# One slot body instead of three, and the remainder moved into short conditional blocks at the slot's end

## The chip, the cores and the metric

One core of one Trainium2 chip runs the kernel. The metric is the device time of one execution in microseconds. TensorE does the matmuls and transposes, VectorE, ScalarE and GpSimd the work between them, SyncE issues most of the weight loads. In the profile their names are PE (PEld for its weight loads), DVE, ACT, POOL and SP; a trailing q means the engine's sequencer, which waits, branches, loads registers and issues DMAs.

## The reference, cut to what matters

Causal attention (2 batches, 12 heads, 448 tokens, head size 64), then a mixture of eight experts in which each token goes to one expert, then a second stage that all 896 tokens go through.

```python
attn = softmax(mask(q @ k.T / 8)) @ v            # -> x: 896 tokens x 768
expert_idx = argmax(cos(x, expert_emb) / tau)    # one expert of 8 for each token
gate_w = probability of that expert
for e in range(8):
    mask = expert_idx == e
    if not mask.any(): continue
    h = maximum(x[mask] @ w1[e], 0)              # w1[e]: 768 x 1024
    out[mask] = gate_w[mask] * (h @ w2[e])       # w2[e]: 1024 x 768
x = out
h = maximum(maximum(x @ m1, x @ m2), x @ m3)     # 768 x 768 each
return h @ m_out
```

## The kernel before

The attention is written out by hand in an order of its own (the strings of `SCHEDULE`) and ends with the routing: a few dozen small VectorE operations on counts, ranks and tables, from which the indices for the gathers and the register values of all later branches come.

The expert stage works in slots of 128 tokens of one expert. Slots 0 and 1 are part of the last `SCHEDULE` string, slot 2 always follows, and slots 3 to 11 stand in nested conditions on the number of slots (`rest3` to `rest11`, line 1230). With these inputs there are seven slots, 0 to 6. A slot multiplies fp32 data as pairs of a high and a low fp32r part: `L1` (x by w1, two halves of 512 columns), a ReLU on ScalarE, transposes of the hidden units (`htr`), `L2` (by w2, two halves of 384), and in the next slot the gate (`yev`, ScalarE, into the tile `y`) and the transposes of the result (`ytr`). While a slot runs, `ws` loads the weights of the next slot's expert and splits them into high and low parts (ScalarE and VectorE), each piece in a condition on the register `need`: the split is left out when the next slot has the same expert.

What remains of an expert's tokens after its full slots, if it is 64 or fewer, becomes a light row of 32 or 64 tokens, computed in plain fp32 from the raw weights. A light row rides in a slot of number 3 or more whose successor needs no new weights, since the buffers for raw weights (six of 768 KB) are free there; rows that find no slot go to up to eight tail blocks (`tail0` to `tail7`, line 1224) between slot 2 and slot 3. Here there are three light rows: 32 tokens in slot 3, 64 in slot 4, 32 in slot 6. Slot 5 is plain and loads weights for slot 6. No tail block runs.

Every slot of number 3 or more is written three times (lines 464 to 470): plain, with a light row of 32, with one of 64. `kind`, two bits of a register that `kinds_load` (line 1194) fills from the table `tabi`, chooses. In the two bodies with a light row its steps stand between the slot's own: `begin` issues six of eight weight loads and gathers the tokens; `x` (token transposes) and `L1` stand ahead of the slot's second `L2` group, `hT` and `L2` after later groups, `out` at the end; the last two weight loads are issued inside `Light.L1` and reuse buffers of the first ones. VectorE computes the tables in `lights` (slot 1) and `lights2` (late in slot 2, hook `(2, 0)`, behind all of the splits of w1 and ahead of those of w2).

Branch hints for `rest4` and on are set in the slot before (`rest_hint`). The program on each engine runs in order; conditions and their register arithmetic are instructions of the engine's queue.

Of the kernel before, what the change touches and what calls it, by code (L numbers as in the profile page):

```python
# [37 lines left out]
def kernel(  # L38
# [15 lines left out]
    nc = tc.nc  # L54
# [60 lines left out]
    k64 = const.tile([P, 14], F32, name="k64")  # L115
# [5 lines left out]
    def consts(tp):  # L121
# [10 lines left out]
        nc.gpsimd.iota(k64, pattern=[[64, 14]], base=0, channel_multiplier=0, allow_small_or_imprecise_dtypes=True)  # L132
# [166 lines left out]
    class Slot:  # L299
# [15 lines left out]
        def regs(self):  # L315
            i = self.i
            if self.prep:
                if i:
                    xg(i + 1)
                if i < 3:  # L320
                    self.needs()
# [62 lines left out]
    class Light:  # L384
        def __init__(self, row, nt):
            self.row, self.nt, self.T = row, nt, P // nt
            self.w = {}

        def begin(self):
            r, nt = self.row, self.nt  # L390
            self.e = nc.values_load(tabi[0:1, T_LE + r:T_LE + r + 1], engines=(ET.SP, ET.Pool), min_val=0, max_val=E - 1)
            self.off = nc.values_load(tabi[0:1, T_LO + r:T_LO + r + 1], engines=(ET.Activation,), min_val=0, max_val=896)
            self.load([(0, p) for p in (0, 2, 1, 3)])
            nc.gpsimd.tensor_copy(out=lix, in_=idx[:, bass.ds(self.e + NH, 1)])
            nc.gpsimd.indirect_dma_start(out=lxr[:nt], out_offset=None, in_=xd, in_offset=bass.IndirectOffsetOnAxis(ap=lix[:nt], axis=0))
            nc.gpsimd.tensor_copy(out=lgt, in_=grep[:, self.T // 4, bass.ds(self.e, 1)])
            self.load([(1, p) for p in (0, 2)])

        def load(self, places):
            for kind, p in places:  # L400
# [72 lines left out]
    def slot_body(S, prev, R):  # L473
        if R:
            R.begin()
        elif S.prep and S.i > 2:
            S.needs()
# [901 lines left out]
```

## Time and profile before

| | us |
|---|---|
| median of 3 runs | 505.13 |
| lowest, highest | 504.69, 509.04 |
| the profiled execution | 505.45 |
| its span, first to last instruction | 503.7 |
| mean granted TensorE clock | 0.959 |
| TensorE busy | 460.2 (91%) |
| VectorE, ScalarE busy | 304.6 (60%), 235.9 (47%) |

The profiled execution takes 505.45 us, of which 503.7 us are the span and 1.75 us lie around it. The granted clock is a share of full speed: 1.00 is 2.4 GHz, 0.50 is 1.2 GHz. Busy time doesn't count branches, register loads, semaphore and DMA-issuing instructions; these are in the views by source line, under a q name (TensorE's under PEldq).

### The profile page before, as it was taken

The page shows a single profiled execution, that of the slowest core. Times are in us where ns is not written, and L with a number is a line of the kernel's source. Part 1 is how long each engine was busy: PE and PEld are TensorE (multiplying, and loading weights), DVE is VectorE, ACT ScalarE, POOL GpSimd, SP SyncE. Part 2 cuts the span into 40 slices and gives each one's busy share as a digit, 9 for nine tenths or more (in the row PEclk, how much of TensorE's full clock was granted, in tenths as well). Part 3 has the DMA queues.
Part 4 walks back from the last instruction along what each step waited for, and adds up shares of the span by engine and source line. Part 5 has one row for each costly group of instructions (what it writes and reads, how often), then busy time and mean ns, then how long its engine had stood idle before and what let it go on. Part 6 is the DMA issues. An engine that isn't in the chain of part 4 may idle for free. (4 is left out here: it accounts for less than half of the span.)

```text
span 503.7 us, 8299 instructions
## 1 busy us (share of the span) xinstructions
PE 460.2 (91%) x2801; PEld 384.7 (76%) x2801; DVE 304.6 (60%) x697; ACT 235.9 (47%) x521; POOL 54.9 (11%) x98
## 2 busy tenths in 40 slices
PE   8899999999899949919999597899999999999994
PEld 6666666776789938718679476699999999999994
DVE  5899868985769891100107420689899898844000
ACT  6768779797359943112128331644344443411000
POOL 5330221111101020100001300000000000000111
PEclk9999999999899979958999799799999999999998
DMA  8754427711159949680549642753355430000111
GB/s 211 202 170 108 120 78 289 299 61 39 31 209 391 391 139 350 223 334 8 188 118 375 234 188 112 308 196 135 116 187 173 141 127 0 1 0 33 62 64 62
DMA packets 28618, 81.52 MB, mean 162 GB/s; under 512 B 13432, under 2 KB 14968, under 8 KB 28544
## 3 DMA queue, kind: packets, MB, share of 16 engines
q1 hardware_dynamic: 25648, 71.46, 40.5%
q0 software_dynamic: 2272, 9.05, 5.3%
q8 instruction: 33, 0.54, 0.5%
q14 instruction: 41, 0.34, 0.2%
q10 hardware_dynamic: 624, 0.14, 0.1%
HBM read 75.13 MB, written 5.51 MB: 160 GB/s over the span
## 5 line engine op out<-in xcount | busy, mean ns | idle before, releaser
L1181 PE MATMUL pm<-x2h,dwh 128*128 128x448 f32 x204 | 74.8, 367 | 0.0
L1182 PE MATMUL pm<-x2l,dwh 128*128 128x448 f32 x204 | 74.8, 367 | 0.0
L1183 PE MATMUL pm<-x2h,dwl 128*128 128x448 f32 x204 | 74.7, 366 | 0.0
L1187 PE MATMUL l<-w1h,xhp 128*128 128x512 f32 x73 | 33.7, 462 | 23.1 <-issue 12.1
L629 PE MATMUL pss<-kt,qbd 128*128 128x320 f32 (+6 forms) x168 | 45.8, 395 | 0.9 <-ACT prb L643 0.8
L643 ACT ACTIVATE prb<-pss,sm 128x64 f32<-128x64 f32 (+6 forms) x84 | 39.5, 484 | 9.5 <-DVE sm L636 9.4
L215 DVE TENSOR_TENSOR hl<-htp,hh 128x512 fp32r<-128x512 f32 x11 | 7.6, 689 | 57.0 <-ACT hh L214 48.1
L1183 PEld LDWEIGHTS pm<-x2h,dwl 128*128 128x128 f32 x204 | 38.3, 188 | 3.4
L1181 PEld LDWEIGHTS pm<-x2h,dwh 128*128 128x128 f32 x204 | 38.3, 188 | 3.4
L1182 PEld LDWEIGHTS pm<-x2l,dwh 128*128 128x128 f32 x204 | 38.3, 188 | 3.3
L1187 PE MATMUL l<-w2h,hh 128*128 128x384 f32 x112 | 40.1, 358 | 0.7 <-ACT hh L218 0.7
L1187 PE MATMUL l<-w2l,hh 128*128 128x384 f32 x112 | 38.3, 342 | 0.0
L182 ACT CAST dwh<-dt_t 128x768 fp32r<-128x768 f32 (+1 forms) x20 | 15.5, 773 | 48.1 <-DVE dt_t L181 48.1
L1187 PEld LDWEIGHTS l<-w1h,xhp 128*128 128x128 f32 x73 | 16.1, 220 | 26.3 <-issue 18.6
L629 PEld LDWEIGHTS pss<-kt,qbd 128*128 128x128 f32 x168 | 28.1, 190 | 9.3 <-ACT prb L643 1.8
L253 DVE TENSOR_TENSOR w1l<-raw,w1h 128x768 fp32r<-128x768 f32 x24 | 21.5, 951 | 20.6 <-PE l L1187 17.5
L636 DVE TENSOR_REDUCE sm<-pss 128x1 f32<-128x448 f32 (+6 forms) x84 | 31.3, 412 | 4.1 <-PE pss L632 3.9
L1187 PE MATMUL l<-w1l,xhp 128*128 128x512 f32 x73 | 32.4, 444 | 0.0
L663 PE MATMUL pst<-ident,prb 128*128 128x128 f32 x192 | 30.0, 281 | 2.1 <-DVE prb L653 1.7
L1333 POOL DMA_INDIRECT out_dram<-ob,sidx x7 | 6.8, 977 | 209.3 <-DVE sidx L1178 177.6
L1187 PE MATMUL l<-w2h,hl 128*128 128x384 f32 x112 | 26.9, 344 | 2.0 <-DVE hl L221 2.0
L1181 PE MATMUL po<-woh,h2h 128*128 128x384 f32 (+2 forms) x84 | 28.2, 335 | 0.0
(330 smaller groups left out, 984.8 us busy)
## 6 DMA issues: line engine op xcount, KB each, us to landing
raw<-in_moe_w_dram SPq DMA_DIRECT2D x56, 768.0 KB, 7.0
rawd<-in_moe_w_dram SPq DMA_DIRECT2D x18, 768.0 KB, 4.7
rawd<-in_moe_w_out_dram SPq DMA_DIRECT2D x6, 768.0 KB, 5.0
vr<-in_v_dram SPq DMA_DIRECT2D x12, 256.0 KB, 2.8
kt<-in_k_dram SPq DMA_DIRECT2D x12, 224.0 KB, 4.6
xd<-xall POOLq DMA_DIRECT2D x12, 224.0 KB, 3.2
qbd<-in_q_dram SPq DMA_DIRECT2D x23, 112.0 KB, 4.5
xrp<-xd,idx POOLq DMA_INDIRECT x8, 6.5
```

Of the source, the lines that this page charges most:

```text
L182: nc.scalar.copy(out=hi[:, c0:c1], in_=f)
L215: nc.vector.tensor_tensor(out=lo, in0=ps_ap, in1=hi, op=ALU.subtract)
L253: nc.vector.tensor_tensor(out=lo[:, sl], in0=r[:, sl], in1=hi[:, sl], op=ALU.subtract)
L629: nc.tensor.matmul(ps[:, o:o + n], lhsT=qbd[p % 4][:, i], rhs=ktt[p][:, :n], start=i == SG[g][0], stop=False, skip_group_check=True)
L636: nc.vector.tensor_reduce(out=sms[p][:, 0, SC[i]:SC[i] + 1], in_=held["s", p, g][:, SO[i]:SO[i] + 64 * (i + 1)], axis=AX.X, op=ALU.max, ne ...
L643: nc.scalar.activation(out=prb[p % 2][:, poff[i]:poff[i] + n], in_=ps[:, SO[i]:SO[i] + n], func=AF.Exp, bias=sm[:, 0, SC[i]:SC[i] + 1], sc ...
L663: nc.tensor.transpose(ps[:, n * P:(n + 1) * P], prb[p % 2][:, poff[i] + kt * P:poff[i] + (kt + 1) * P], ident)
L1181: nc.tensor.matmul(o, lhsT=lh, rhs=rh, start=first, stop=False)
L1182: nc.tensor.matmul(o, lhsT=lh, rhs=rl, start=False, stop=False)
L1183: nc.tensor.matmul(o, lhsT=ll, rhs=rh, start=False, stop=last)
L1187: nc.tensor.matmul(o, lhsT=a, rhs=b, start=first and n == 0, stop=last and n == len(ops) - 1)
L1333: nc.gpsimd.indirect_dma_start(out=out, out_offset=bass.IndirectOffsetOnAxis(ap=sidx[:, t:t + 1], axis=0), in_=ob, in_offset=None)
```

## The change

Each slot now has one body. A slot of number 3 or more gets a `Light` object that shares the slot's eight raw buffers. `begin` stands at the slot's start in a condition of its own on SyncE and GpSimd alone (six loads, the gather of always 64 tokens, two copies of gates); the transposes of the tokens (`x`) are done in every such slot, of rows that a memset on GpSimd filled with zeros once; the copy of their result is in a condition on VectorE. The rest moves to the slot's end, behind the last `L2` group: `sizes(L1)`, then `rest` (the last two loads, a condition on SyncE), then `sizes(tail)` (`hT`, `L2`, `out` in a row). `sizes` is a condition on TensorE, ScalarE and VectorE, and in it a choice between 32 and 64 tokens. The slot's own conditional weight splits stay in every body. `kinds_load` loads the register four times, for four groups of engines, and `needs` is loaded in each slot. `lights2` moves from hook `(2, 0)` to `(2, 3)`, ahead of the last four splits of w1. Of the routing's small operations two leave the first chain for `lights`, `g64` halves, and `selL` is new.

```diff
-    k64 = const.tile([P, 14], F32, name="k64")
+    k64 = const.tile([P, 7], F32, name="k64")
...
     class Light:
-        def begin(self):
-            r, nt = self.row, self.nt
-            self.e = nc.values_load(tabi[...T_LE + r...], engines=(ET.SP, ET.Pool), ...)
-            self.off = nc.values_load(tabi[...T_LO + r...], engines=(ET.Activation,), ...)
-            self.load([(0, p) for p in (0, 2, 1, 3)])
-            nc.gpsimd.tensor_copy(out=lix, in_=idx[:, bass.ds(self.e + NH, 1)])
-            nc.gpsimd.indirect_dma_start(out=lxr[:nt], ..., in_=xd, in_offset=...lix[:nt]...)
-            nc.gpsimd.tensor_copy(out=lgt, in_=grep[:, self.T // 4, bass.ds(self.e, 1)])
-            self.load([(1, p) for p in (0, 2)])
+        def begin(self, nt=64):
+            r = self.row
+            for place in self.first:
+                self.w[place] = self.raw_of(*place)
+            with self.ride("s", nt):
+                self.e = nc.values_load(tabi[...T_LE + r...], engines=(ET.SP, ET.Pool), ...)
+                for place in self.first:
+                    wdma(self.e, *place, self.w[place])
+                nc.gpsimd.tensor_copy(out=lix, in_=idx[:, bass.ds(self.e + NH, 1)])
+                nc.gpsimd.indirect_dma_start(out=lxr, ..., in_=xd, in_offset=...lix[:64]...)
+                for t in range(2):
+                    nc.gpsimd.tensor_copy(out=lgt[:, t:t + 1], in_=grep[:, t, bass.ds(self.e, 1)])
+
+        first = [(0, 0), (0, 1), (0, 2), (0, 3), (1, 0), (1, 2)]
+        last = [(1, 1), (1, 3)]
+
+        def rest(self):
+            for place in self.last:
+                self.w[place] = self.raw_of(*place)
+            with self.ride("s"):
+                e = nc.values_load(tabi[...T_LE + self.row...], engines=(ET.SP,), ...)
+                for place in self.last:
+                    wdma(e, *place, self.w[place])
+
+        def ride(self, engines, nt=0):
+            if self.row >= NL:
+                return ExitStack()
+            return tc.If(self.kind(engines) > 0)
+
+        def kind(self, engines):
+            return (rest["k" + engines] // 4 ** self.row) % 4
+
+        def sizes(self, part):
+            ...
+            with tc.If(self.kind("c") > 0):
+                with tc.If(self.kind("c") == 1) as small:
+                    self.nt, self.T = 32, 4
+                    part()
+                with small.Else():
+                    self.nt, self.T = 64, 2
+                    part()

         def x(self):
             pb = bank("t", "lxt", 3)
             for k in range(KD):
-                nc.tensor.transpose(pb[:, k * nt:(k + 1) * nt], lxr[:nt, ...], ident[:nt, :nt])
-            nc.vector.tensor_copy(out=sp["y"][:, :KD * nt], in_=pb[:, :KD * nt])
+                nc.tensor.transpose(pb[:, k * 64:(k + 1) * 64], lxr[:, ...], ident[:64, :64])
+            with self.ride("v"):
+                nc.vector.tensor_copy(out=sp["y"][:, :KD * 64], in_=pb[:, :KD * 64])
...
             nc.scalar.activation(out=hp0[:, :f], in_=pb[:, :f], func=AF.Relu)
-            self.load([(1, p) for p in (1, 3)])
...
+        def tail(self):
+            self.hT()
+            self.L2()
+            self.out()
...
     def slot(i, prep, prev):
-        kind = (rest["k"] // 4 ** (i - 2)) % 4
-        with tc.If(kind == 0, preferred_fallthrough_block=True) as plain:
-            slot_body(S, prev, None)
-        with plain.Else():
-            with tc.If(kind == 1, preferred_fallthrough_block=True) as small:
-                slot_body(S, prev, Light(i - 2, 32))
-            with small.Else():
-                slot_body(S, prev, Light(i - 2, 64))
+        slot_body(S, prev, Light(i - 2, S.raw_of) if i > 2 else None)
...
     def slot_mid(S, R=None):
...
-        if R:
-            R.x()
         S.L2(0, range(4))
         S.htr(1)
         hook(i, -1)
...
-        if R:
-            R.L1()
-        ws(0, (2, 0), (2, 1))
+        hook(i, 3)
+        S.ws(0, (2, 0), (2, 1))
         S.L2(1, range(4))
-        if R:
-            R.hT()
-        ws(0, (3, 0))
+        S.ws(0, (3, 0))
         S.L2(0, range(4, 8))
-        if R:
-            R.L2()
-            hook(i, 2)
-        ws(0, (3, 1))
+        S.ws(0, (3, 1))
         hook(i, 0)
...
-        ws(1, (0, 0), (0, 1))
+        if R:
+            R.x()
+        S.ws(1, (0, 0), (0, 1))
         S.L2(1, range(4, 8))
-        ws(1, (2, 0), (2, 1), (1, 0), (1, 1), (3, 0), (3, 1))
+        S.ws(1, (2, 0), (2, 1))
+        if R:
+            hook(i, 2)
+            R.sizes(R.L1)
+            R.rest()
+            R.sizes(R.tail)
+        S.ws(1, (1, 0), (1, 1), (3, 0), (3, 1))
         if i == 2:
             hook(i, 2)
-        if R:
-            R.out()
         hook(i, 1)
...
     lxr = lxw[:64]
+    nc.gpsimd.memset(lxr, 0.0)
...
     def kinds_load():
-        rest["k"] = nc.values_load(tabi[...T_KIND...], min_val=0, ...)
+        for g, engines in (("", None), ("c", (ET.PE, ET.Activation, ET.DVE)), ("s", (ET.SP, ET.Pool)), ("v", (ET.DVE,))):
+            kw = {"engines": engines} if engines else {}
+            rest["k" + g] = nc.values_load(tabi[...T_KIND...], min_val=0, ..., **kw)
...
-    hooks[2, 0] = lambda: lights2()
+    hooks[2, 3] = lambda: lights2()
```

## Rows read from the trace of the kernel before

**Rows 1.** Stretches: us, busy us (instructions) of each engine, granted clock, DMA share, GB/s

```profile
178.00:185.10 7.10, 0.11 (x2) 0.02 (x1) 7.00 (x25) 3.81 (x5) 2.10 (x2) 0.81 0.09 35
185.10:213.70 28.60, 28.12 (x227) 22.85 (x227) 6.31 (x12) 5.78 (x13) 4.29 (x8) 0.93 0.78 273
213.70:224.70 11.00, 0.00 (x0) 0.00 (x1) 0.00 (x0) 1.96 (x6) 0.37 (x2) 0.63 0.93 349
224.70:258.50 33.80, 33.77 (x172) 23.94 (x173) 3.56 (x6) 5.08 (x10) 1.17 (x2) 0.92 0.28 101
258.50:277.60 19.10, 19.06 (x107) 17.21 (x105) 10.47 (x14) 13.89 (x24) 2.35 (x3) 1.00 0.86 310
277.60:281.60 4.00, 0.00 (x0) 0.00 (x0) 4.00 (x6) 4.00 (x7) 2.19 (x1) 0.97 0.61 198
281.60:311.50 29.90, 28.88 (x227) 23.34 (x227) 4.82 (x8) 4.87 (x11) 1.77 (x1) 0.89 0.50 193
311.50:317.30 5.80, 0.03 (x2) 0.03 (x1) 0.56 (x2) 1.57 (x6) 0.00 (x0) 0.85 0.02 6
```

**Rows 2.** Branches on TensorE's queue, by source line and window: ns shortest/median/longest, starts

```profile
L464 PEldq COMPARE_BRANCH  x1: 2505/2505/2505, 182.2 to 182.2; - x1
...
L464 PEldq COMPARE_BRANCH  x1: 4432/4432/4432, 212.5 to 212.5; - x1
...
L467 PEldq COMPARE_BRANCH  x2: 386/3861/7336, 211.7 to 217.2; - x2
...
L372 PEldq COMPARE_BRANCH  x1: 6217/6217/6217, 274.3 to 274.3; - x1
...
L1228 PEldq COMPARE_BRANCH  x2: 203/1798/3392, 313.0 to 316.6; - x2
```

**Rows 3.** Stretches in slot 0, columns as in Rows 1

```profile
124.00:127.70 3.70, 1.01 (x6) 0.45 (x4) 3.41 (x18) 1.06 (x2) 0.34 (x11) 1.00 0.00 0
127.70:131.50 3.80, 3.80 (x26) 3.49 (x27) 1.95 (x6) 1.15 (x2) 0.00 (x0) 0.55 0.00 0
```

**Rows 4.** GpSimd's groups by line and form: busy us, mean ns of one

```profile
L570 POOL MEMSET qbd<- 64x448 f32 x6 | 3.0, 493 | 0.2
```

**Rows 5.** VectorE's timeline: start, us, line, operation

```profile
124.15 0.27 DVE L97 TENSOR_TENSOR lxw<-n8p,k 128x112 f32<-128x112 f32 x1
...
176.84 0.45 DVE L97 TENSOR_TENSOR lxw<-enT,v 128x288 f32<-128x288 f32 x1
...
180.51 0.18 DVE L1146 CAST tabi<-tabf 1x56 int32<-1x56 f32 x1
...
206.21 0.42 DVE L432 COPY lhT<-lht 128x256 f32<-128x256 f32 x1 [3.64 <-PE lht L431]
```

**Rows 6.** ScalarE's timeline: start, us, line, operation, [idle before <- what ended it]

```profile
189.34 1.05 ACT L291 ACTIVATE y<-l,gs 128x384 f32<-128x384 f32 x2 [6.93 <-DVEq L1222]
...
203.82 0.38 ACT L424 ACTIVATE hp<-ll 128x256 f32<-128x256 f32 x1 [2.15 <-PE ll L414]
...
211.19 0.42 ACT L443 ACTIVATE hp<-ll,lgt 128x192 f32<-128x192 f32 x1 [6.99 <-PE ll L414]
```

**Rows 7.** Register loads of line 1195 on VectorE's queue: ns, start

```profile
L1195 DVEq TENSOR_LOAD <-tabi x1: 320/320/320, 188.2 to 188.2; - x1
```

**Rows 8.** TensorE's timeline: start, us, line, operation

```profile
193.28 0.82 PE L296 MATMUL ytp<-ident,y 128*128 128x128 f32 x6
...
200.88 2.80 PE L414 MATMUL ll<-raw,y 128*32 128x256 f32 x48
...
208.21 2.81 PE L414 MATMUL ll<-raw,lhT 128*32 128x192 f32 x64
...
240.68 5.37 PE L414 MATMUL ll<-raw,y 128*64 128x512 f32 x24
```

**Rows 9.** SyncE's timeline, the late two loads of slot 3's light row

```profile
202.40 0.91 SPq L247 DMA_DIRECT2D raw<-in_moe_w_dram  x2
```

**Rows 10.** The microsecond in which they finish, columns as in Rows 1

```profile
207.00:208.00 1.00, 1.00 (x8) 0.96 (x6) 0.00 (x0) 0.00 (x0) 0.00 (x0) 1.00 0.72 283
```

More of the change, by code (lines that the diff above doesn't have):

```diff
@@ L319, in regs @@
                     xg(i + 1)
-                if i < 3:
-                    self.needs()
+                self.needs()
         def needs(self):
@@ L399, in load, with __init__ @@
-        def load(self, places):
-            for kind, p in places:
-                self.w[kind, p] = wraw()
-                wdma(self.e, kind, p, self.w[kind, p])
+        def __init__(self, row, raw_of=None):
+            self.row, self.w = row, {}
+            self.raw_of = raw_of or (lambda kind, u: wraw())
+        def begin(self, nt=64):
[3 more added lines that the diff above has]
+            with self.ride("s", nt):
+                self.e = nc.values_load(tabi[0:1, T_LE + r:T_LE + r + 1], engines=(ET.SP, ET.Pool), min_val=0, max_val=E - 1)
+                for place in self.first:
+                    wdma(self.e, *place, self.w[place])
+                nc.gpsimd.tensor_copy(out=lix, in_=idx[:, bass.ds(self.e + NH, 1)])
+                nc.gpsimd.indirect_dma_start(out=lxr, out_offset=None, in_=xd, in_offset=bass.IndirectOffsetOnAxis(ap=lix[:64], axis=0))
+                for t in range(2):
+                    nc.gpsimd.tensor_copy(out=lgt[:, t:t + 1], in_=grep[:, t, bass.ds(self.e, 1)])
@@ new lines @@
+        first = [(0, 0), (0, 1), (0, 2), (0, 3), (1, 0), (1, 2)]
[4 more added lines that the diff above has]
+            with self.ride("s"):
+                e = nc.values_load(tabi[0:1, T_LE + self.row:T_LE + self.row + 1], engines=(ET.SP,), min_val=0, max_val=E - 1)
+                for place in self.last:
[4 more added lines that the diff above has]
+            return tc.If(self.kind(engines) > 0)
@@ new lines, in kind @@
+        def kind(self, engines):
+            return (rest["k" + engines] // 4 ** self.row) % 4
+        def sizes(self, part):
+            if self.row >= NL:
+                self.nt, self.T = 64, 2
+                part()
+                return
+            with tc.If(self.kind("c") > 0):
[3 more added lines that the diff above has]
+                with small.Else():
+                    self.nt, self.T = 64, 2
+                    part()
@@ L475, in slot_body @@
             R.begin()
-        elif S.prep and S.i > 2:
-            S.needs()
         S.L1(0, range(6))
@@ L486, in slot_body @@
         prev.ytr(1)
-        if not R:
-            S.ws(0, (0, 0))
+        S.ws(0, (0, 0))
         S.htr(0)
@@ L493, in slot_mid @@
         i = S.i
-        def ws(*a):
-            if not R:
-                S.ws(*a)
         if i == 1:
-            ws(0, (0, 0))
-        ws(0, (0, 1))
+            S.ws(0, (0, 0))
+        S.ws(0, (0, 1))
         if i > 1:
             S.L1(1, range(3, 6))
-        ws(0, (1, 0))
+        S.ws(0, (1, 0))
         if i > 1:
             S.relu(1)
-        ws(0, (1, 1))
-        if R:
-            R.x()
+        S.ws(0, (1, 1))
         S.L2(0, range(4))
@@ L917 @@
     lix = rtile([P, 1], "lix", I32)
-    lgt = rtile([P, 1], "lgt")
+    lgt = rtile([P, 2], "lgt")
     grep = rtile([P, 2, E], "grep")
@@ L921 @@
     n8 = rtile([P, E], "n8")
-    g64 = lview(160, 112).rearrange("p (e k) -> p e k", e=E)
-    nbs = rtile([P, 2, E], "nbs")
-    nb8, nh8 = nbs[:, 0], nbs[:, 1]
+    g64 = lview(160, 56).rearrange("p (e k) -> p e k", e=E)
+    nh8 = rtile([P, E], "nh8")
     pre8 = rtile([P, E, E], "pre8")
@@ L1224 @@
             es.enter_context(tc.If(rest["k"] >= 4 ** NL * (t + 1), preferred_fallthrough_block=True, label=f"tail{t}"))
-            L = Light(NL + t, 64)
-            for part in (L.begin, L.x, L.L1, L.hT, L.L2, L.out):
-                part()
+            L = Light(NL + t)
+            L.begin()
+            L.x()
+            L.sizes(L.L1)
+            L.rest()
+            L.sizes(L.tail)
     with ExitStack() as es:
```

43 lines of the change are left out of this document (18 added, 25 removed), and 2 rows, old and new, of the table SCHEDULE.

## The prediction

> **What bounds the kernel now.** I read the windows by stage first, for the stretch that the change touches, 178 to 317 us: it begins where TensorE has finished slot 2 and ends where the second stage begins. Look at TensorE's column and at the clock [rows 1]. TensorE is the bound in slot 5 (19.06 of 19.1 us busy) and within the other slots, but four stretches hold almost none of it: 7.1 us ahead of slot 3, 11.0 ahead of slot 4, 4.0 ahead of slot 6, 5.8 ahead of the second stage, 27.9 us in all. Slots 3, 4 and 6 also run at mean clocks of 0.93, 0.92 and 0.89. If the lower level is half speed, the time lost is (1 - clock) x length: 2.0, 2.7 and 3.3 us.
>
> Then the branches by source line say what fills the gaps [rows 2]. The choice of body (L464, L467) held TensorE's queue for 2.5 us ahead of slot 3 and for 4.4 and 7.3 us ahead of slot 4. The jump from the end of the plain body of slot 5 over two unused bodies (under L372) took 6.2 us, of which some 3 lay under matmuls already queued. The exit (L1228) took 3.4 us. A plain body is some 210 TensorE instructions long (107 matmuls and 105 weight loads in slot 5 [rows 1]), one with a light row longer, and these branches jump over one or two of them. A branch of the same kind at 211.7 took 0.39 us and one at the exit 0.2, so the length of a jump is not all: a long branch is taken here as one whose target was not there yet.
>
> The gap ahead of slot 3 has two other late comers. VectorE writes the integer table at 180.5 to 180.7, 3.9 us after it began the tables at 176.84 [rows 5], and TensorE can't know its branches before. And ScalarE's `y` of slot 2, whose transposes TensorE does 8.2 us into slot 3 (193.28 [rows 8]), waits until 189.34 for VectorE to pass the tail blocks [rows 6].
>
> **The change, part by part.** The sum is made against the profiled execution, 505.45 us (span 503.7 and 1.75 around it); the median of the runs, 505.13, is 0.3 lower. Plus is slower.
>
> *Routing.* The memset of 64x768 scales from 64x448 in 0.49 us [rows 4] to 0.85 us, an estimate. GpSimd does it ahead of its other small work there, and the first VectorE write to that tile (`g64`, 124.15 [rows 5]) has to wait for it. Two small operations leave this chain; the smallest row of VectorE here lasts 0.18 us [rows 5], so they give some 0.3 back. The memset ends half a microsecond or so after `g64` could begin: I take +0.3, bounds 0 and +0.9. The three operations added in `lights` lie under TensorE's slot 1 and cost nothing; without that cover they would cost 3 x 0.18.
>
> *Entry of slot 3.* Tables 3.9 us earlier and no choice of body: TensorE's first matmul can come just after 178, say at 179.1 with the added register load. Its work up to the transposes of `y` took 8.2 us, 6.2 without the slow clock, so it stands at them at 185.3. VectorE has the same operations in another order and is busy without a break (7.00 of 7.1 us [rows 1]), so it comes to the tail blocks no earlier, and it has two more register loads of 0.32 us each, 0.4 with what surrounds them [rows 7]. `y` is then begun at 190.1 and transposed from 190.8 instead of 193.28: -2.5. TensorE has waited 5.5 us for it and starts at the low clock again. Even short waits do that: after two gaps that left 1.0 us of work in 3.7, the clock was 0.55 for 3.8 us [rows 3]. So the 2.0 us that slot 3 loses now are lost again, behind the transposes: -0.5 in all, bounds -2.5 and +1. What is late next is VectorE's splitting, and the tables' earlier place buys next to nothing.
>
> *The light rows of 32 (slots 3 and 6).* Today each step stands between groups of the slot's own matmuls. At the end of the slot nothing is left to cover them, and TensorE waits for each hand-over. Behind `L1`: ReLU 0.22 us after the last matmul, 0.38 long, 0.2 back to TensorE, 0.8 [rows 6, 8]. Behind the transposes of `hT`: a copy of 0.42 us, 0.66 with the hand-over [rows 5]. Behind `L2`: the gate, 0.42 us, 0.8 [rows 6]. The last two weight loads: issued at 202.40, half-way through `L1` [rows 8, 9], they moved their last bytes 0.72 into the microsecond from 207 [rows 10], 5.35 us after the issue. In the new body they stand behind a condition, so I let them start when `L1` ends; `L2`, with 0.8 + 0.4 + 0.66 us and its first half of 1.4 ahead of it, needs them after 3.2 us: 2.1 us of waiting. Branch and register instructions not hidden, 0.4. That is +4.8 for each row, bounds +2.7 (loads half-way through `L1`, as now) and +7 (the low clock after it). SyncE's next loads, those of the following slot, queue behind the two late ones, and nobody needs them for 19 us.
>
> *The light row of 64 (slot 4).* `L1` takes 5.37 us [rows 8] and `L2` as long, so the loads come in time (0.15 us of waiting); the three hand-overs are wider, 1.0, 0.9 and 1.0; 0.5 for branches: +3.6, bounds +3 and +5.6.
>
> *Entry of slot 4.* Of 11.0 us 0.5 stays: -10.5. Of 2.7 us of low clock I keep 1.0 for what the chain of slot 3 may leave: -1.7.
>
> *Slot 5 and entry of slot 6.* Token transposes without use, 0.55 us, and branches, 0.4: +1.0. The jump of 6.2 us goes: the gap of 4.0, 1 us of idle time and 2.3 of low clock inside slot 6 go with it, less 0.3 for branches: -7.0. `y` is no limit there: ScalarE, busy to the end of the gap, is through with it 23 us after slot 5 began [rows 1], and TensorE asks for it after 19.1 + 1.0 + 6.2 = 26.3.
>
> *Exit.* The jump from the 32-row body over the 64-row one, ahead of the exit's own jump, goes; the 3.4 us of the exit stay: -1.2, bounds -4.5 (its hint works with fewer jumps between) and 0.
>
> *Joins.* A consumer behind a conditional block waits for the end of the producer's block, not for its instruction. No row shows what that adds; I take a second hand-over of 0.2 us, as above, for three in each of three chains: +1.8, bounds 0 and +3. The unused conditions of `ws` in light slots are on ScalarE, VectorE and SyncE, which idle for most of such a slot (5.78 and 6.31 us busy of 28.6 [rows 1]); in an engine without that slack each would cost its branch.
>
> Sum: 0.3 - 0.5 + 2 x 4.8 + 3.6 - 10.5 - 1.7 + 1.0 - 7.0 - 1.2 + 1.8 = -4.6. That gives 500.9 for a profiled execution, 500.5 against the median.
>
> **The rivals.**
>
> *The skips in slot 5 miss (504.5).* A slot with no light row jumps over the code of `L1` (48 matmuls of the one size and 24 of the other, each with a weight load, 144 instructions) and at once over the tail (about 216 more). Rows show jumps of this length both ways: 0.39 us, and 2.5 to 6.2 [rows 2], the longest while weight loads filled the DMA queues, as they do in slot 5 (share 0.86 [rows 1]). Half of a 6 us hold is hidden by queued matmuls; the rest, and some 2 us of low clock behind it, cost 4 to 5. The Trainium skill ("Runtime: NRT & Kernel Launch", section "Instruction fetch mechanics") says that a taken branch to a target outside the current two pages of 256 instructions stalls for a fetch; by that rule this pair of skips, 360 instructions, leaves the window from a little under half of all positions. The same section gives TensorE room for 2048 instructions, by which none of the long branches should have been; the trace speaks against that figure.
>
> *The chains are short (494).* The two late loads start half-way through `L1` (2 x -2.1), the clock holds, the exit's hint works (-3.4 at most). For it: full clock inside the light rows today. Against it: a condition on SyncE stands between.
>
> *Slower: the chains are bound by the late loads (511).* If the following slot's loads, whose buffers come free at the same moment, share the queues with the two late ones, four loads of 2 us each and the start of 1.3 make them land 9.4 us behind `L1` instead of 5.4: +4 in each of three chains, with 2 us of low clock each, less what the sum holds already: about +10 over the forecast. It decides from the point where `L2`'s second half waits for more than some 3 us. Against it: SyncE issues the late ones first.
>
> *The jumps stay (505).* The conditions at the end of a slot could miss as often as the bodies did. Against it: most of the jumps that are left are a quarter as long.
>
> **How the numbers follow.** Forecast 0.42, with 497 to 503.5 as its own range; skips miss 0.25; short chains 0.18; late loads 0.09; jumps stay 0.06. One per cent is 5 us, about what a measurement of this kernel can tell from no change. Faster by more than that (under 500.1): not quite half of the forecast (0.19), nearly all of the short chains (0.17), a fifth of the missed skips, with cheaper chains (0.05): 0.41. Slower: the late loads and a little of the two cases that end near 505: 0.11. The range takes in most of the short chains and the missed skips: 492 to 508.
>
> **What would show it.** In the profile after: no TensorE branch of over 1 us ahead of slots 3 and 4; slot 3's `y` transposes near 191 with `y` still released by VectorE at the tail blocks; in each light row three idle times of 0.7 to 1.0 us on TensorE, and one of about 2 us in the second half of `L2` of the 32-row ones; slot 4 beginning near 218. I am wrong if the gaps stay, if TensorE runs on through the light rows, or if a skip in slot 5 holds its queue.

## The result and the profile after

The changed kernel takes 502.49 us (median of 20 runs, 498.29 to 507.75) against 506.54 for the kernel before beside it (20 runs, 504.53 to 510.62): ratio 0.990, 95% interval 0.987 to 0.993, 3.7 to 6.4 us less. That ratio leaves out the three slowest runs of the changed kernel (506.35 to 507.75), which are more than 1.5% above its fastest; the two medians alone give 0.992, or 4.1 us less. The prediction said 500.5 against 505.13, or 4.6 less. Timed once more with other kernels the ratio was 0.9925 (0.9895 to 0.9955). The total came out near the forecast. In the profiles the stretch that the prediction is about gave only two thirds of it, though, and a place that it did not look at gave much of the rest; both are shown below.

The changed kernel's profiled execution took 499.93 us (span 498.2), 5.5 less than that of before; it is one of the shorter of its 20 runs. Its stretches, cut where its slots begin and end, in the columns of [rows 1]: us, busy us of each engine, granted clock, DMA share, GB/s.

```profile
178.60:191.60 13.00, 6.72 (x28) 5.02 (x28) 10.28 (x14) 3.89 (x7) 3.79 (x7) 0.98 0.54 187
191.60:203.70 12.10, 12.10 (x65) 11.34 (x65) 2.31 (x4) 4.38 (x9) 1.19 (x2) 0.88 0.79 277
203.70:219.00 15.30, 11.35 (x137) 6.87 (x136) 0.98 (x2) 0.81 (x2) 0.93 (x1) 0.89 0.61 215
219.00:253.00 34.00, 31.59 (x175) 22.14 (x174) 3.56 (x6) 7.16 (x16) 1.66 (x5) 1.00 0.49 180
253.00:274.20 21.20, 19.93 (x112) 17.58 (x110) 12.17 (x16) 14.18 (x24) 3.57 (x5) 1.00 0.57 208
274.20:283.10 8.90, 6.57 (x28) 5.02 (x28) 3.73 (x5) 3.69 (x6) 0.69 (x1) 1.00 0.87 312
283.10:311.30 28.20, 23.60 (x200) 18.09 (x200) 3.86 (x7) 5.10 (x11) 0.00 (x0) 0.88 0.48 188
311.30:314.50 3.20, 0.03 (x1) 0.00 (x0) 0.62 (x2) 1.53 (x6) 0.00 (x0) 0.93 0.19 40
```

The empty stretches of [rows 1] are gone. In their place each slot with a light row has TensorE busy for less than its length, and 283.10 to 311.30 has a clock of 0.88. Cut finer, the low clock of slots 3 and 6 lies in four short stretches: behind the two waits at 191.58 and 283.07 (the first is in the second row above), and at the end of the two light rows of 32.

```profile
215.10:219.00 3.90, 3.27 (x32) 1.62 (x32) 0.00 (x0) 0.42 (x1) 0.00 (x0) 0.57 0.95 364
...
283.10:287.00 3.90, 3.90 (x15) 3.37 (x16) 1.26 (x2) 2.35 (x5) 0.00 (x0) 0.56 1.01 411
287.00:307.30 20.30, 16.43 (x155) 13.11 (x153) 2.60 (x5) 2.33 (x5) 0.00 (x0) 1.00 0.47 182
307.30:311.30 4.00, 3.26 (x31) 1.61 (x31) 0.00 (x0) 0.42 (x1) 0.00 (x0) 0.59 0.03 6
```

TensorE's branches show why the empty stretches went; the groups answer to [rows 2] (ns shortest/median/longest, starts).

```profile
L425 PEldq COMPARE_BRANCH  x4: 68/72/83, 203.9 to 240.0; - x4
...
L426 PEldq COMPARE_BRANCH  x8: 66/187/337, 204.3 to 252.6; - x8
...
L425 PEldq COMPARE_BRANCH  x2: 334/554/773, 270.3 to 273.1; - x2
...
L1249 PEldq COMPARE_BRANCH  x2: 186/322/459, 311.1 to 311.7; - x2
```

No branch lasts 0.8 us where those of [rows 2] lasted 2.5 to 7.3. TensorE's timeline shows what it waits for now, and answers to [rows 8] (start, us, line, operation, [idle before <- what ended it]).

```profile
179.64 0.49 PE L1203 MATMUL l<-w1h,xhp 128*128 128x512 f32 x1 [1.08 <-ACT w2h L252]
191.58 1.54 PE L296 MATMUL ytp<-ident,y 128*128 128x128 f32 x6 [4.80 <-ACT y L291]
...
209.89 0.44 PE L459 MATMUL lht<-ident,hp 128*128 128x128 f32 x2 [0.60 <-ACT hp L453]
210.84 1.51 PE L443 MATMUL ll<-raw,lhT 128*32 128x192 f32 x32 [0.52 <-DVEq L371]
213.17 0.52 PE L443 MATMUL ll<-raw,lhT 128*32 128x192 f32 x4 [0.82 <-DMA raw<-in_moe_w_dram]
215.07 2.78 PE L443 MATMUL ll<-raw,lhT 128*32 128x192 f32 x28 [1.38 <-DMA raw<-in_moe_w_dram]
218.49 0.52 PE L484 MATMUL lyt<-ident,hp 128*64 128x128 f32 x3 [0.63 <-ACT hp L471]
218.97 0.49 PE L1203 MATMUL l<-w1h,xhp 128*128 128x512 f32 x1
...
245.03 0.63 PE L459 MATMUL lht<-ident,hp 128*128 128x128 f32 x4 [0.83 <-issue]
246.45 5.38 PE L443 MATMUL ll<-raw,lhT 128*64 128x384 f32 x32 [0.78 <-DVEq L371]
252.62 0.55 PE L484 MATMUL lyt<-ident,hp 128*128 128x128 f32 x3 [0.79 <-ACT hp L471]
...
274.23 0.49 PE L1203 MATMUL l<-w1h,xhp 128*128 128x512 f32 x1 [1.30 <-PEq L425]
283.07 1.38 PE L296 MATMUL ytp<-ident,y 128*128 128x128 f32 x6 [2.29 <-ACT y L291]
302.52 1.51 PE L443 MATMUL ll<-raw,lhT 128*32 128x192 f32 x32 [0.52 <-DVE lhT L460]
304.99 0.52 PE L443 MATMUL ll<-raw,lhT 128*32 128x192 f32 x4 [0.96 <-SPq L1249]
307.40 2.77 PE L443 MATMUL ll<-raw,lhT 128*32 128x192 f32 x28 [1.90 <-SPq L1249]
314.51 0.74 PE L1203 MATMUL pm<-x2h,dwh 128*128 128x448 f32 x1 [3.19 <-ACT x2h L214]
```

Slot 3 begins at 179.64, stands at `y` until 191.58, and slot 4 begins at 218.97. The hand-overs of the light rows take 0.5 to 0.8 us each; `L2` of 32 rows waits twice in its course for the late loads. The row at 283.07 is a wait that was not forecast: slot 6 stands 2.29 us at the transposes of `y`. SyncE's longest wait for TensorE's queue leads to its cause (us in total, times, longest):

```profile
SPq L247 <- PEq L425: 10.0, 1, 10.0
```

SyncE, in slot 5, wants to issue the last two weight loads for slot 6 (places 1 and 3 of w2) and waits 10.0 us, until 274.05. That is 0.09 us after TensorE's semaphore instruction behind the last jump, the one over the unused tail (273.96). The loads land behind the start of slot 6, and ScalarE splits them before it comes to `y`:

```profile
279.14 1.57 ACT L252 CAST w2h<-raw 128x768 fp32r<-128x768 f32 x2 [6.65 <-DMA raw<-in_moe_w_dram]
280.98 1.56 ACT L252 CAST w2h<-raw 128x768 fp32r<-128x768 f32 x2 [0.26 <-DMA raw<-in_moe_w_dram]
282.45 1.05 ACT L291 ACTIVATE y<-l,gs 128x384 f32<-128x384 f32 x2
```

A ledger by stretch, from the start of the first matmul of each slot in the two traces (the first stretch begins where slot 2's last matmul ends: 178.10 before, 178.56 after). The column "predicted" holds the prediction's terms of that stretch, its joins at 0.6 for each chain. The last is a second profiled execution of the changed kernel, e10 below.

| stretch | before | after | difference | predicted | e10 |
|---|---|---|---|---|---|
| end of slot 2 to slot 4 | 46.63 | 40.41 | -6.2 | -5.6 | 40.44 |
| slot 4 | 33.81 | 34.00 | +0.2 | +2.5 | 34.26 |
| slot 5, to slot 6 | 23.09 | 21.26 | -1.8 | -2.7 | 21.18 |
| slot 6, to the second stage | 35.65 | 40.28 | +4.6 | +0.9 | 40.25 |
| sum | 139.18 | 135.95 | -3.2 | -4.9 | 136.13 |

The remaining -2.7 of the profiled difference lie behind 314.5, in the second stage, whose program the change does not touch; ahead of the end of slot 2 there is +0.5.

### The profile page after: what moved, and what is told of

Read it like the earlier page. It is cut to its first block, busy times and chain, and to the rows that moved or that the text cites. A ratio compares the mean times of both kernels' runs of the same rounds, so it can differ in the third digit from the quotient of the medians.

```text
span 498.2 us, 8666 instructions
## 1 busy us (share of the span) xinstructions
PE 458.9 (92%) x2807; PEld 381.6 (77%) x2807; DVE 305.7 (61%) x699; ACT 236.3 (47%) x521; POOL 53.0 (11%) x102
## 5 line engine op out<-in xcount | busy, mean ns | idle before, releaser
L1203 PE MATMUL l<-w2h,hh 128*128 128x384 f32 x112 | 39.1, 349 | 0.7 <-ACT hh L218 0.7
L1203 PE MATMUL l<-w1h,xhp 128*128 128x512 f32 x73 | 30.6, 420 | 2.8 <-PEq L425 1.3
L1203 PE MATMUL l<-w1l,xhp 128*128 128x512 f32 x73 | 29.4, 403 | 0.0
L1197 PE MATMUL po<-woh,h2h 128*128 128x384 f32 (+2 forms) x84 | 28.2, 335 | 0.0
L1199 PE MATMUL po<-woh,h2l 128*128 128x384 f32 (+2 forms) x84 | 28.1, 335 | 0.0
L1198 PE MATMUL po<-wol,h2h 128*128 128x384 f32 (+2 forms) x84 | 28.1, 335 | 0.0
```

The lines of the kernel that those rows point to most:

```text
L1197: nc.tensor.matmul(o, lhsT=lh, rhs=rh, start=first, stop=False)
L1198: nc.tensor.matmul(o, lhsT=lh, rhs=rl, start=False, stop=False)
L1199: nc.tensor.matmul(o, lhsT=ll, rhs=rh, start=False, stop=last)
L1203: nc.tensor.matmul(o, lhsT=a, rhs=b, start=first and n == 0, stop=last and n == len(ops) - 1)
```

## The experiments

**Tables where they were, in the changed kernel** (e1).

```diff
-    hooks[2, 3] = lambda: lights2()
+    hooks[2, 0] = lambda: lights2()
```

> The changed kernel with the tables computed behind the last four splits of w1 again, as before. My theory (TensorE in slot 3 waits for y, which waits for VectorE at the tail blocks, whatever the order of VectorE's work): TensorE's first matmul of slot 3 comes some 3 us later (about 183), its wait ahead of the y transposes shrinks from 4.8 to about 2 us, the transposes stay within 0.7 us of where they are, and the time is that of the changed kernel within 1 us (ratio to before 0.99). Rival (the earlier tables are a main part of the gain): 3 us more than the changed kernel, ratio 0.996.

Ratio to the kernel before 0.9956 (0.9928 to 0.9984). By the total the tables seem to be worth 0.3 to 0.6%, against the changed kernel's second and first timing, and the ratio is the one that the rival named; the trace puts the difference elsewhere.

```profile
182.74 0.79 PE L1203 MATMUL l<-w1h,xhp 128*128 128x512 f32 x1 [4.49 <-ACTq L1240]
191.18 1.01 PE L296 MATMUL ytp<-ident,y 128*128 128x128 f32 x6
```

Slot 3 starts 3.1 us later than in the changed kernel, at low clock, and its transposes of `y` come at 191.18 without a wait, against 191.58. What the early tables win is lost in waiting for `y`, as the prediction said. The stretch from slot 2 to the second stage takes 137.00 us against 135.95, and 0.9 of the 1.05 us lie at the exit, where TensorE stands still for 4.10 us instead of 3.19; its branch took 3.34 us here and 0.46 in the changed kernel's first profile. The interval overlaps with that of the changed kernel's second timing, so the totals do not decide; the trace speaks for the theory.

**Tables alone, in the kernel before** (e2).

```diff
+        hook(i, 3)
         ws(0, (2, 0), (2, 1))
...
-    hooks[2, 0] = lambda: lights2()
+    hooks[2, 3] = lambda: lights2()
```

> The kernel before with nothing but the tables moved ahead of the last four splits of w1. TensorE still takes the jump to the light body (2.5 us), so slot 3 starts near 181.5 instead of 185.1; y is begun at 189.3 as before, so its transposes come at 190.0 to 190.5 instead of 193.3. My theory: 2 to 3 us less than before there, ratio 0.994 to 0.996; the gaps ahead of slots 4 and 6 as before. Rival (the low clock or VectorE takes all of it back): ratio 1.0.

Ratio 1.002 (0.9992 to 1.0049), the rival's. The transposes of `y` in slot 3 come at 191.45, 1.8 us earlier than [rows 8]; ahead of slot 4 all of it is lost, since the branches there take as long as before or longer:

```profile
L464 PEldq COMPARE_BRANCH  x2: 2565/3853/5141, 179.3 to 211.9; - x2
...
L467 PEldq COMPARE_BRANCH  x3: 78/300/7713, 182.2 to 217.3; - x3
```

So the tables alone gain nothing, and the long branches go only where the bodies go.

**Hints for the choice of body, in the kernel before** (e6): could the long branches have been mended without the change?

```diff
-        with tc.If(kind == 0, preferred_fallthrough_block=True) as plain:
+        with tc.If(kind == 0, preferred_fallthrough_block=True, label=f"plain{i}") as plain:
...
+    def kind_hint(i):
+        k = (rest["k"] // 4 ** (i - 2)) % 4
+        tc.mark_branch_hint_location(f"plain{i}", (4 - k) // 4, engines=(ET.PE,))
+        tc.mark_branch_hint_location(f"small{i}", (3 - k) // 2, engines=(ET.PE,))
```

> The kernel before with branch hints for TensorE on the choice of body in slots 4 and on, set in the slot before. If the long branches are jumps to code that was not there, and a hint brings it in time: the 4.4 and 7.3 us ahead of slot 4 shrink below 1 us each, the gap of 11 us to 1 to 4, and the time falls by 7 to 11 us, ratio 0.978 to 0.986; the jump at the end of slot 5 has no hint and stays. Rival (the hint is not acted on, or the code comes no earlier, because the DMA queues are full of weights): ratio 0.998 to 1.002, branches as long as before.

Ratio 1.0031 (1.0003 to 1.0058), near the rival's. The branches are as long as without hints, in a profiled execution that is the longest of the twelve (513.03 us):

```profile
L467 PEldq COMPARE_BRANCH  x2: 4912/5492/6072, 217.9 to 224.9; - x2
...
L372 PEldq COMPARE_BRANCH  x1: 6997/6997/6997, 278.8 to 278.8; - x1
```

The hints for slot 4 stand at 216.8 and 217.3 in TensorE's queue, 1 us ahead of the first of its two long branches and 8 us ahead of the second; the jump at the end of slot 5 has none. Whether hints set earlier would shorten them was not tried.

**The light parts spread over the slot again, in one body** (e3): each step in a condition of its own between the slot's matmuls, and the first six weight loads of a slot without a light row in one condition at the slot's start.

```diff
         if R:
             R.begin()
+            S.preload(R.first)     # one If(need > 0) around six wdma
...
+        if R:
+            R.x()
         S.L2(0, range(4))
...
+        if R:
+            R.sizes(R.L1)
+            R.rest()
         S.ws(0, (2, 0), (2, 1))
         S.L2(1, range(4))
+        if R:
+            R.sizes(R.hT)
         S.ws(0, (3, 0))
         S.L2(0, range(4, 8))
+        if R:
+            R.sizes(R.L2)
+            hook(i, 2)
...
-            R.sizes(R.L1)
-            R.rest()
-            R.sizes(R.tail)
...
+            R.sizes(R.out)         # at the end
```

> The changed kernel with one body and conditions, but the light steps back between the slot's own matmuls: x ahead of L2, L1 ahead of the second L2 group, then hT, L2 and out each in a condition of its own at its old place; the weight loads of a plain slot are issued in one condition at its start. If the hand-overs at the slot's end and the late loads are what the change pays (idle time of 3.9, 2.4 and 4.6 us in the three chains, 2.3 us for y in slot 6, and some 4 us of low clock): 489 to 494, ratio 0.965 to 0.977. Rival (the price of the change lies in the conditions themselves, and more of them in the middle of a slot cost more): 502 or more.

493.46 us, ratio 0.976 (0.9721 to 0.9799). The price of the chains at the end of a slot is real. Slot 6, to the second stage, takes 33.76 us against 40.28, slot 4 31.45 against 34.00. Slot 3 wins nothing (41.69 from the end of slot 2, against 40.41): its `L1` stands still for 3.48 us.

```profile
205.33 5.39 PE L452 MATMUL ll<-raw,y 128*32 128x256 f32 x48 [3.48 <-SPq L380]
```

L380 is the new condition around the six loads, which this slot skips. The loads of the light row itself had been issued ahead of it; the fourth, the last of w1, landed at 201.34 and the sixth at 205.08, and SyncE's semaphore behind the skipped condition released TensorE at 205.2. So `L1` waited for all six loads, though it reads four; in e8, which lacks the condition, it does not wait. `y` in slot 6 still makes TensorE wait 1.62 us, and the late loads of its light row 1.60, but here the clock stays high through the slot:

```profile
273.60:304.20 30.60, 27.34 (x227) 21.45 (x227) 8.26 (x12) 8.77 (x16) 0.00 (x0) 1.00 0.66 246
```

**Only `x`, `L1` and the late loads spread, the tail at the end** (e7), and **e3 without its one condition around six loads** (e8).

```diff
 e7, against e3:
-            R.sizes(R.hT)
...
-            R.sizes(R.L2)
...
+            R.sizes(R.tail)        # at the end
 e8, against e3:
-            S.preload(R.first)
```

> The changed kernel with the token transposes, L1 and the two late loads of each light part moved back to the middle of the slot, and the first six weight loads of a slot without a light row put in one condition ahead of L1; the tail (hT, L2, out) stays at the slot's end. Theory (the wait for y at the entry of slot 6, 2.3 us and 2 to 3 us of low clock behind it, comes from two weight loads that wait for TensorE to pass the unused L1, and the late loads cost what they showed, 2.2 us in each row of 32): both go, as do three hand-overs of 0.5 to 0.8 us, some -11 us; the L1 of slot 3 now waits for its own weights as it did with everything spread, +3.5 and some low clock. Ratio to the kernel before 0.978 (0.973 to 0.984), y transposes in slot 6 without a wait of over 1 us, no wait on raw in L2. Rival (the three hand-overs of the tail and the joins behind them carry what spreading gave): ratio 0.985 to 0.990, as the changed kernel.

> The spread kernel without the one condition that holds the first six loads of a slot without a light row: each load stands again behind its own condition, most of them behind the conditional L1. Theory (what holds SyncE's loads in a slot without a light row is the conditional light part that it may not pass before TensorE has): four loads of slot 5 are issued only when TensorE has passed the unused L1, and the wait for weights or y in slot 6 comes back, 2 to 6 us: ratio to the kernel before 0.981 to 0.988. Rival (SyncE passes an unused block at once, and only shared buffers hold it): as the spread kernel, 0.974 to 0.979.

e7: 493.46 us, ratio 0.9733 (0.9708 to 0.9758). e8: 497.62, ratio 0.982 (0.9785 to 0.9855). SyncE's wait for TensorE's queue and the transposes of `y` in slot 6, in e7:

```profile
SPq L247 <- PEq L434: 9.3, 1, 9.3
```

```profile
279.53 1.02 PE L296 MATMUL ytp<-ident,y 128*128 128x128 f32 x6 [2.71 <-ACT y L291]
```

The total of e7 lies at the lower end of what the theory said, but its first half fell: the wait for `y` in slot 6 is still there (with the clock at 1.00 behind it). TensorE had passed the unused `L1` at 263.36, and SyncE waited 9.3 us all the same, to 270.07, 0.08 after TensorE had passed the unused tail. So it is not `L1` that holds the loads. These two loads write the very tiles (places 1 and 3 of w2, shared through `raw_of`) that `L2` in the tail reads, and they stand behind the tail in the program. In e8 four loads stand behind the conditional `L1`, SyncE waits 16.2 us in two parts, and slot 6 stands 5.79 us at `y`; the wait came back as the theory there said. The interval of e8's total touches that of e3.

**The two last loads issued ahead of the tail**, in e7 (e11) and ahead of the conditional `L2` in e3 (e12). In a slot that loads weights no light row rides, so nothing that runs reads these tiles in between.

```diff
             R.rest()
+            S.preload(R.last)
         S.ws(0, (2, 0), (2, 1))
```

> The kernel with the light L1 in the middle of the slot and the tail at its end, and now the two last weight loads of a slot without a light row (places 1 and 3 of w2) are issued ahead of the tail, in one condition behind the two late loads of the light part. In the kernel without this they waited 9.3 us until TensorE had passed the unused tail (270.0; it had passed the unused L1 at 263.4), and y in slot 6 was waited for 2.7 us. Theory (a load into a buffer that the conditional tail reads, behind the tail in program order, waits for TensorE to pass the tail even where it is jumped over): the loads are issued near 263.5 to 264.5, the wait for y in slot 6 falls below 0.7 us, and with it some 2 us of low clock: ratio to the kernel before 0.962 to 0.968, against 0.973. Rival (the wait was for L1's buffers, or the splits of these loads wait for something else at the slot's end, such as TensorE's own use of w2): y stays late by over 2 us and the ratio at 0.971 to 0.976.

> The spread kernel with the same two loads issued ahead of the conditional L2. There they waited until TensorE had passed the unused L2 (270.6); it had passed the unused L1 at 265.7. Theory: issued near 266, y in slot 6 waits for less than 0.7 us instead of 1.6: ratio to the kernel before 0.966 to 0.973, against 0.976. Rival (as for the other kernel): no change, 0.974 to 0.979. It also says again whether tail at the end or spread is better: by the runs so far, 0.973 against 0.976, the tail at the end is not worse.

e12: 488.82 us, ratio 0.9692 (0.9631 to 0.9753), the best version of the study, in 4 runs whose interval still overlaps with e3's. e11: 494.85, ratio 0.979 (0.9747 to 0.9834), no better than e7, outside what theory and rival said.

```profile
SPq L247 <- PEq L436: 2.7, 1, 2.7
```

```profile
271.46 0.49 PE L1220 MATMUL l<-w1h,xhp 128*128 128x512 f32 x1 [0.32 <-PEq L436]
...
277.84 0.82 PE L296 MATMUL ytp<-ident,y 128*128 128x128 f32 x6
...
301.26 0.47 PE L1220 MATMUL pm<-x2h,dwh 128*128 128x448 f32 x1 [3.14 <-ACT x2h L214]
```

```profile
271.40:301.20 29.80, 26.66 (x227) 21.56 (x227) 9.00 (x13) 9.98 (x22) 0.00 (x0) 1.00 0.58 214
```

These are e12's waits of SyncE, TensorE's timeline and the stretch of slot 6. SyncE waits 2.7 us instead of 7.6, `y` is there when TensorE comes to it, the clock holds at 1.00 through slot 6 as it did in e3, and slot 6 takes 29.80 us to the second stage against 33.76 in e3. Of these 4.0 us 1.62 are the wait for `y` and 1.60 that for the late loads, the last of which lands 22.5 us behind the slot's start instead of 26.4. The mechanism is shown in the traces: the loads waited for a block that was jumped over, and `y` waited for the loads. In e11 `y` is in time too (278.52, no wait), but the jump over the whole tail, now with loads under way, holds TensorE's queue:

```profile
L436 PEldq COMPARE_BRANCH  x2: 216/2469/4722, 261.3 to 267.0; - x2
```

```profile
272.14 0.49 PE L1217 MATMUL l<-w1h,xhp 128*128 128x512 f32 x1 [1.87 <-ACT w2h L252]
```

**The changed kernel again, and without TensorE's hints for the slots** (e10, e9).

```diff
-        hooks[i - 1, 0] = lambda i=i: rest_hint(i, ET.PE, ET.Pool, ET.SP)
+        hooks[i - 1, 0] = lambda i=i: rest_hint(i, ET.Pool, ET.SP)     # e9 alone
```

> The changed kernel once more, beside the others. Theory: ratio to the kernel before 0.987 to 0.993; the profile shows the wait for y in slot 6 (2.0 to 2.6 us), waits for the late loads of 2.0 to 2.6 us in each row of 32, and the exit's branch at 0.5 us again. Rival (the exit's short branch was luck of one execution): the exit's branch holds TensorE some 3.4 us with everything else alike.

> The changed kernel without the TensorE branch hints of the slots (4 in the executed slots, the last of them for the exit). Theory (the hint makes the exit's branch short: 0.46 us in the changed kernel): the exit's branch holds TensorE 3.3 to 3.5 us, and the time is 2 to 3 us longer: ratio to the kernel before 0.994 to 0.997. Rival (whether the target is there depends on where the code lies, not on the hint): the branch stays at 0.5 us or is as long in some kernels with the hint too, ratio 0.988 to 0.992.

e10: ratio 0.9925 (0.9895 to 0.9955). e9: 0.9944 (0.9915 to 0.9973). The exit's branch, e10 first, then e9:

```profile
L1249 PEldq COMPARE_BRANCH  x2: 191/1586/2980, 313.1 to 316.3; - x2
```

```profile
L1249 PEldq COMPARE_BRANCH  x2: 186/2574/4961, 312.7 to 317.9; - x2
```

The 0.46 us of the changed kernel's first profile was one execution's luck, as the rival said: 2.98 us in e10 with the same program. Without the hint it was 4.96, but the two totals overlap, so what the hint is worth stays open. Up to some 3 us it matters little here: with a branch of 0.46 us TensorE stood still for 3.19 us at the exit, with 2.98 us for 3.41, released both times by ScalarE's first split of x2; with e9's 4.96 us it was 5.69. `y` in slot 6 waited 1.84 us in e10, the late loads 2.2 and 3.1: the rest repeats.

**The place of the tiles** (e13, e14). The second stage was shorter after the change, and not in one place. Over 110 us with TensorE busy throughout, matmuls of one shape took 367 ns before and 364 after (busy us, mean ns):

```profile
L1182 PE MATMUL pm<-x2l,dwh 128*128 128x448 f32 x180 | 66.0, 367 | 0.0
```

```profile
L1198 PE MATMUL pm<-x2l,dwh 128*128 128x448 f32 x183 | 66.6, 364 | 0.0
```

Told apart in units of 18 matmuls, which take the two halves of the tokens in turn, it is every second one: 17 units take 206.0 ns from start to start before, 200.5 after; the units between them take 202.7 and 202.6. The halves lie in pools on the two sides of SBUF, the first on the left. The change made `k64` smaller, by which nearly every tile of the left side moved by 32 bytes per partition; the right side did not move. An unused tile puts that back (e13), or moves the kernel before the other way (e14).

```diff
     k64 = const.tile([P, 7], F32, name="k64")      # e14: [P, 14], the kernel before
+    pad = const.tile([P, 8], F32, name="pad")
+    nc.gpsimd.memset(pad, 0.0)
```

> The changed kernel with one unused tile of 32 bytes per partition beside k64, which the change made 28 bytes per partition smaller: nearly every tile of the left pools lies 32 bytes further on again, where it lay in the kernel before; the programs on the engines stay as they are, but for one small memset at the start. In the second stage the kernels without the change's layout had 17 units of 18 matmuls (x2h and x2l of the first half of the tokens) at 206 to 207 ns from start to start, those with it at 200 to 202: 17 x 18 x 5.7 ns = 1.7 us that no step of the prediction holds. Theory (the tiles' place in SBUF sets it): those units go back to 206 ns, the second stage's matmuls last 179.5 to 180.1 us instead of 177.3 to 178.4, and the ratio to the kernel before rises by 0.003 to 0.005, to 0.993 to 0.997. Rival (it is something else in the changed program): 200 ns, 177.3 to 178.4 us and 0.988 to 0.993.

> The kernel before with the same unused tile of 32 bytes per partition: nothing else is changed, and the tiles of the left pools lie 32 bytes further on, at the same remainder by 64 bytes as in the changed kernel. Theory: the units of the first half go from 206 to 200 ns, the second stage's matmuls last 177.3 to 178.4 us instead of 180, and the ratio is 0.994 to 0.997. Rival (the layout has no part in it, or the remainder by 64 does not decide): 1.000 within 0.003, 180 us.

e13: ratio 0.9973 (0.9948 to 0.9998). The 17 units are back at 206.0 ns, and the stage's matmuls last 180.19 us, against 177.30 in the changed kernel and 180.02 before.

```profile
L1200 PE MATMUL pm<-x2l,dwh 128*128 128x448 f32 x180 | 66.0, 367 | 0.0
```

So the place of the tiles sets it, and 17 x 18 x 5.5 ns = 1.7 us of the changed kernel's gain come from a small tile of the routing. The expectation puts the 17 units on the first half of the tokens. By the program's order, first half first, they are on the second: their own operand on the right side did not move, and the weights on the left, which did, are those of the units between them too. Which pair of places makes the difference is open. e14 is only half as clear: its units fall to 202.6 ns and the stage to 178.83 us, as the theory had it in direction, but the total is 1.0039 (1.0007 to 1.0071), not faster. Its trace has the stretch from slot 2 on 0.7 us longer and slot 2 ending 1.15 us later; whether that is the layout's price elsewhere or one execution's is open. Three places gave three pitches (200.5, 206.0, 202.6 ns), so the remainder by 64 bytes is not the rule.

## Why the prediction came out

**The gaps by branches: right.** All of the long holds of [rows 2] ahead of slots 3, 4 and 6 are gone, and e2 and e6 show that neither the tables nor hints set in the slot before do that. The rivals that the skips in slot 5 miss and that the jumps stay did not come about in the changed kernel: 0.33 and 0.77 us in its profile, 0.34 and 0.69 in e10.

**Entry of slot 3: right.** Predicted: first matmul 179.1, transposes of `y` 190.8, low clock behind them. Measured: 179.64, 191.58 after a wait of 4.80, clock 0.88 over the 12.1 us behind it, or 1.5 us lost where 2.0 were forecast. In the place of [rows 6]'s row stands `y` at 190.94. e1 shows that the early tables buy nothing as long as `y` comes then.

**The light rows of 32: right in size, not in every part.** Hand-overs 0.8 + 0.66 + 0.8 were forecast, 0.60, 0.52 and 0.63 measured; the late loads 2.1 against 2.2 (0.82 and 1.38 in slot 3; 2.9 in slot 6), though from their issue to the end of the wait 6.1 us passed in slot 3 (208.97 to 215.07) where the forecast has 5.35; its own rows give 5.32. The low clock behind the loads, which the forecast has only in its upper bound, came in both rows: 0.57 over 3.9 us and 0.59 over 4.0, 1.7 and 1.6 us. So the idle time and the low clock make 5.7 and 6.2 us, against 4.8 and 0.6 for joins; the 1.0 us for branches and joins does not show. Slot 4 began at 218.97 where 218 was said. e3 and e12 show from the other side what the chains cost.

**The light row of 64: sized too high.** +2.5 for the slot, with the clock won back, +0.2 measured. The hand-overs were 0.83, 0.78 and 0.79 instead of 1.0, 0.9 and 1.0, no load was waited for, and the clock was 1.00 throughout, where 1.0 us of low clock had been kept; the joins' 0.6 does not show.

**Entry of slot 6: the step that failed.** "`y` is no limit there" compared ScalarE's time to get through with TensorE's 26.3 us, taken from slot 5 as it was [rows 1]. It did not ask which loads ScalarE's splits wait for in the new order. The light parts were moved to the end of the slot, two loads of the plain slot stand behind them, and those share the tiles that the unused tail reads; SyncE, a queue that the step was moved past, waits for TensorE to pass it. ScalarE ended `y` 30.5 us after slot 5 began, not 23. That is a wait of 2.29 us, 1.84 in e10, with a clock of 0.56 over the 3.9 us behind it, 1.7 us lost, the same in e10. The other half of the slot's low clock, (1 - 0.88) x 28.2 = 3.4 us, is that of the light row above. Of the -7.0 the gap gave 2.8 (4.07 to 1.30). Of the 1.0 us of idle time and 2.3 of low clock that were to go, slot 6 gave back 0.3: it stands still for 2.29 us where it had stood for 0.99, and loses 1.7 us of the 3.3 again behind that wait. e11 and e12 take the wait away. How long the wait is does not decide the clock alone: behind 1.62 us in e3 and 2.71 in e7 it stayed at 1.00. With the light row and the exit below this leaves some 1.3 us of slot 6's +4.6 in no term.

**Exit: mis-sized by a little.** The jump between the bodies went and the other stayed, as forecast; the gap fell from 5.8 to 3.2 and 3.4 us, -2.4 to -2.6 against -1.2.

**Late loads as the bound: not so.** `L2` waited 2.2 to 3.1 us for them in the two profiles of the changed kernel; the longest, in slot 6 of e10, is at the 3 us from which that rival decides, but the 10 us that it forecast did not come.

**Routing: not told apart.** +0.3 was forecast, and slot 2 ended 0.46 us later. But over the profiles with the old routing (e2, e6, e14 beside the kernel before) its end lies anywhere from 178.10 to 181.85.

**Not in the sum at all.** The 1.7 us of the tiles' place. Without it the changed order is worth 0.0 to 0.5% (e13), and the traces say 2.7 to 3.2 us for the stretch (e13's is 136.51). The rest of that execution's 2.7 us lies in the stage's first 10 us (45 matmuls begun against 40; 42 in e10), right behind the exit's low clock. The total came out where it was predicted because the tiles gave about as much as the sum was too hopeful by, 4.9 - 3.2 = 1.7 us. That is luck.

**A wait of slot 2** for `y` (1.44 us at 165.40 in the changed kernel, 2.18 in e10) is absent from the profile of before; but e2 and e6, which have the old routing, show 1.61 and 1.70 there. It does not need the change.

The Trainium skill ("Runtime: NRT & Kernel Launch", section "Instruction fetch mechanics") says that a taken branch out of the current two pages stalls for a fetch. The runs agree in kind: jumps over the tail's 216 or so instructions took 0.5 to 0.9 us in five profiles of the changed order (e1, e9, e10, e13 and the first), and 2.5 and 4.7 in e7 and e11. No run shows where the pages lie.

## What to carry to other kernels

A conditional block that is jumped over still held its buffers here until the engine that would have read them had come past it: before moving such a block to the end of a stage, list the loads of the other path that write the same tiles and issue them ahead of it (in slot 6 of e12's profile 4.0 us less than in e3's). Merge bodies so that jumps are short, but leave the optional work spread between the main work's instructions: merged alone gave 0.8 to 1.0% here, merged and spread with the loads ahead 3.1%. And when a change shifts tiles, compare the pitch of identical matmuls in a stage that it does not touch, before its gain is booked to the change.

## What the hardware showed that was not expected

- Matmuls of one shape at full clock took 200.5, 202.6 or 206.0 ns from start to start, depending on where the tiles lay in SBUF, with 32 bytes per partition between one place and the next. The units that changed read the half of the tokens whose tiles had not moved.
- One jump of one program at the same place took 0.46 us in one execution and 2.98 in another, with the DMA queues busy for 0.19 and 0.03 of the time, so a short branch in one profile says little.
- The longest jump over an unused block in slot 5 held TensorE's queue 1.5 us in e3, 2.5, 3.3 and 4.7 us in e7, e8 and e11, and 0.5 to 0.9 in five profiles of the changed order; whether the loads under way or the place of the code makes the difference was not told apart. In e12, with four short jumps in slot 5, each took 0.43 us or less.
